# Attention, mixture of experts and feed-forward on one core: the first expert's first tile computed inside attention's last steps

## The chip, the cores and the metric

The kernel runs on one core of a Trainium2 chip. The metric is the device time of one execution in microseconds (us), the median of several runs. A core has five engines that run side by side, each through its own list of instructions in order: PE (TensorE, the matrix engine), DVE (VectorE), ACT (ScalarE), POOL (GpSimd) and SP (which here only issues transfers). They meet by semaphores. Transfers between the chip's memory and the core's on-chip memory go by 16 DMA engines.

## What is computed

The reference has three parts, one behind the other, cut here to what matters.

```python
# q, k, v: 4 batches, 8 heads, 576 positions, 64 wide
scores = scale * np.matmul(q, k.transpose(0, 1, 3, 2))
kth = np.partition(scores, -32, axis=-1)[..., -32:-31]
scores = np.where(scores >= kth, scores, -1e9)          # the 32 largest of each row
x = softmax(scores) @ v                                  # -> 2304 tokens x 512

do_compute = x @ w_skip > 0                              # the other tokens pass unchanged
e_idx = argmax(x @ w_gate); gate = its softmax           # one of 8 experts for each token
y = gate * (np.maximum(x @ w1[e], 0) @ w2[e])            # 512 -> 1024 -> 512
x[do_compute] += y

h = x @ w_in                                             # 512 -> 2048, weights in float64
out = (h / (1 + np.exp(-1.702 * h))) @ w_out             # 2048 -> 512
```

On the inputs of the reference the experts get 131, 62, 182, 117, 161, 178, 89 and 93 tokens.

## The kernel before

**Attention** is a software pipeline of 144 steps (`NTL`), nine to a pair of heads, sixteen pairs; a step works on one 128-row tile of scores, and its stages (scores, the top-32 threshold on VectorE, mask, transposes, the product with V, normalisation) run a few steps behind one another. The order of the instructions is the order in which the code of a step is written; nothing reorders them. Fourteen further steps (up to `NTL + AVL + 4`, `AVL` is 10) empty the pipeline. The gate of a batch (scores of the eight experts and of the skip weight, tile of 128 tokens by tile) is computed while the next batch is in work. The last batch has none behind it: `last_gate` computes its scores tile by tile in these last steps (transpose L547, copy L549, matmul L551, addition L553).

**Placing.** `rank` (L634, L636) counts on PE for each token how many tokens of its expert come before it. `place` (L642 on) turns that into a row and a column of a list, as one-hot rows `hr` and columns `hc`; `lists` (L703, first three batches, full lists) and `short_lists` (L716, last batch) multiply them on PE, so that each expert's list of token numbers comes out. `LST` collects the lists. For the last batch this is a serial chain between PE and VectorE, with the operations of `order` (the experts sorted by their number of rows, L787 to L812) woven between those of `place`, and nine matmuls on ones (`warm`, L259) on PE. When the first expert's list is there (L718, `IX0`), `first_rows` gathers its rows. Two tiles of 128 and 64 rows hold what an expert can have in the first five places (`BIGS`, "long", up to `NS` = 192 rows), one tile of 128 in the others.

**The flag.** `fine` (L927) is loaded by every engine from the on-chip memory: it is 1 if no expert has too many rows and no threshold was doubtful. Else an If (L1008) computes the lists exactly. Each engine waits behind the If until its branch is taken.

**Experts.** They run in the order of their places, `turns`, 0, 4, 1, 5, 2, 3, 6, 7, a long one and a short one by turns. Expert 0 is always in place 0 (its entry of `tie` is a large number). For an expert, `turn` (L1078) transposes the gathered rows; `layer1` (L1091) does 8 f x 4 fp32 matmuls, with ACT (L1092) and VectorE (L1094) splitting the hidden rows into a high and a low part; `split_w2` (L1136, L1137) splits the second weights likewise; `layer2` (L1109) does three fp32r matmuls for each f, or two where a tile has 64 rows (high and low part side by side); `scatter` writes rows back. Between the layers the next expert's rows are transposed, and the FFN's weights `w_in` are split in sixteen pieces (`split_f64`, L1033 to L1035 on VectorE): `take(e)` hands three pieces to a long expert's time, one to a short one's.

**The feed-forward part** (`L1264`, `L1279`) follows from about 619 us on.

Of the kernel before, what the change touches and what calls it, by code (L numbers as in the profile page):

```python
# [29 lines left out]
def body(ctx: ExitStack, tc: tile.TileContext, q, k, v, w_skip, w_gate, w1, w2, w_in, w_out, out):  # L30
# [82 lines left out]
    IXG = cst.tile([P, 2], I32, name="IXG")  # L113
    ZD = dram.tile([P, 8], F32, name="ZD")
# [6 lines left out]
    def first_rows(ready=False):  # L121
        w, src = (DM, X2D) if ready else (DM + 1, XD)
        if not ready:
            V.tensor_copy(IX0, IDX[:, :2])
            gate_places()
        fetch_rows(x0[0][:, :w], IX0[:, :1], src)
        fetch_rows(x0[1][: NS - P, :w], IX0[: NS - P, 1:], src)
# [4 lines left out]
    def first_gates():  # L132
        one = XD.rearrange("r (w o) -> (r w) o", o=1)
        fetch_rows(x0[0][:, DM:], IXG[:, :1], one)
        fetch_rows(x0[1][: NS - P, DM:], IXG[: NS - P, 1:], one)

    with ExitStack() as ph:
# [15 lines left out]
        IOF = X[:, 2 * P + LW + 8 : 2 * P + LW + 8 + 2 * E]  # L153
# [384 lines left out]
        def last_gate(r, u):  # L538
# [6 lines left out]
            zt, zg = SS[:, r * P : r * P + rows], SS[:rows, 1024 + 9 * r : 1033 + 9 * r]  # L545
# [52 lines left out]
        def gating_last(b):  # L598
# [24 lines left out]
            G.tensor_scalar(cb, wm, -float(NTT), float(E * NTT), op0=ALU.mult, op1=ALU.add)  # L623
# [15 lines left out]
        def place():  # L639
            b, cb = st.pop("fin")  # L640
            W = V if b == B - 1 else G
# [6 lines left out]
            W.tensor_tensor(acc, acc, MS[:, :5, :], op=ALU.mult)  # L648
# [6 lines left out]
            W.tensor_tensor(left, tk, pos, op=ALU.subtract)  # L655
            ad = gm.tile([P, 4, 5], F32, name="ad")
            W.tensor_scalar(ad[:, 0, :], pos, 1.0 / P, -0.498, op0=ALU.mult, op1=ALU.add)
            if W is V:
                yield
            W.tensor_scalar(ad[:, 0, :], ad[:, 0, :], 3.0 * 2.0 ** 22, 1.0, op0=ALU.add, op1=ALU.mult)  # L660
            if W is V:
                yield
            W.tensor_scalar(ad[:, 0, :], ad[:, 0, :], -3.0 * 2.0 ** 22, 1.0, op0=ALU.add, op1=ALU.mult)
            yield
            neg = gm.tile([P, 5], F32, name="neg")
            W.tensor_scalar(neg, ad[:, 0, :], -float(P), 0.0, op0=ALU.mult, op1=ALU.add)
            yield
            W.tensor_tensor(ad[:, 2, :], ad[:, 0, :], cb[:, :, 0], op=ALU.add)
            W.tensor_tensor(ad[:, 3, :], left, neg, op=ALU.subtract)
            W.tensor_tensor(ad[:, 1, :], neg, pos, op=ALU.add)  # L670
            if W is not V:
                yield
            hot = [gm.tile([P, P], F32R, name="hr", bufs=5) for t in range(5)]
            for t in range(3, 5):
                if W is V:
# [681 lines left out]
```

## Time and profile before

| | before |
|---|---|
| median of 3 runs | 1039.68 us (1033.44, 1039.68, 1041.09) |
| profiled execution, own time | 1033.63 us |
| its span in the trace | 1030.7 us |
| mean granted clock of PE | 0.988 |
| PE busy | 989.4 us (96%), 6499 matmuls |
| weight loads of PE | 842.9 us (82%) |
| DVE busy | 704.6 us (68%) |
| ACT busy | 593.1 us (58%) |
| POOL busy | 478.3 us (46%) |

A busy share is a mean over the stages, and the stages have different limits. A row of the timeline names start, length, engine, line, operation, the tile written and the tiles read, shapes and how many instructions it stands for; in brackets stands how long the engine idled before it and what ended that. [...] A plain fp32 matmul is two PE instructions in the trace, and an fp32r one is one. The execution's own time is 2.9 us longer than its span.

### The profile page before, as it was taken

Reading aid. Unit: us, or ns where it says so; the run is one execution under the profiler, and the core shown is the slowest. Engines: PE = TensorE matmul, PEld = TensorE weight load, DVE = VectorE, ACT = ScalarE, POOL = GpSimd, SP = SyncE. Lnnn points to the kernel's source line nnn. Section 1 sums busy time; section 2 is a strip of 40 time slices with the busy share of each in tenths; the row PEclk is TensorE's granted clock in tenths of the full one; section 3 lists DMA queues with packets and bytes.
Section 4 is the critical chain, followed back from the end, with each engine's and each line's share of the span. In section 5 each row is a group of like instructions: output and inputs, shape, how many; then the busy total and the mean of one; then the engine's idle time right before and its main releaser. Section 6 shows DMA issues by size and latency. Waiting matters only on the chain.

```text
span 1030.7 us, 20024 instructions
## 1 busy us (share of the span) xinstructions
PE 989.4 (96%) x6499; PEld 842.9 (82%) x6499; DVE 704.6 (68%) x3326; ACT 593.1 (58%) x1261; POOL 478.3 (46%) x598
## 2 busy tenths in 40 slices
PE   7999999999999999878999989999999999999998
PEld 4888888888888888757989877888888888888887
DVE  7999999999999999965898976653232323322222
ACT  6999999999999999823534533332222222222222
POOL 5788888978898879733765652220000000000000
PEclk9999999999999999998999999999999999999999
DMA  3121116161511151037889863312000200100000
GB/s 87 44 45 38 33 37 130 40 203 40 132 40 40 40 125 24 1 95 281 276 328 385 301 218 134 102 62 73 10 1 1 82 1 1 62 1 1 9 33 21
DMA packets 99010, 92.11 MB, mean 89 GB/s; under 512 B 71760, under 2 KB 71760, under 8 KB 98896
## 3 DMA queue, kind: packets, MB, share of 16 engines
q1 hardware_dynamic: 96704, 83.91, 26.8%
q0 software_dynamic: 1760, 5.25, 1.5%
q10 hardware_dynamic: 432, 1.57, 0.4%
q8 instruction: 53, 0.87, 0.4%
q14 instruction: 61, 0.50, 0.2%
HBM read 72.38 MB, written 17.32 MB: 87 GB/s over the span
## 4 chain that ended last, share of the span: by engine, by line
PE 71%; DVE 18%; DMA 4%; ACT 3%; issue 2%; POOL 1%; another core or an unknown queue 1%; SPq 0%; DVEq 0%; ACTq 0%; POOLq 0%
PE ph L1279 19%; PE py L1264 18%; PE Y L430 7%; DVE C L296 5%; PE SS L273 5%; PE pt L370 4%; DVE z L329 2%; DMA raw<-in_moe_w_in_dram 2%; PE ph L1091 2%; PE pt L371 2%; PE SS L275 2%; PE py L1109 2%; DVE w2l L1137 1%; PE Y L427 1%; PE SS L267 1%
## 5 line engine op out<-in xcount | busy, mean ns | idle before, releaser
L296 DVE MAX8 C<-s 128x8 f32<-128x72 f32 x1152 | 222.0, 220 | 2.2 <-ACT s L289 2.2
L324 POOL TENSOR_TENSOR z<-s,z 128x576 f32<-128x576 f32 x144 | 203.3, 1412 | 43.3 <-ACT z L319 41.1
L1267 DVE TENSOR_TENSOR g<-py,g 128x512 f32<-128x512 f32 (+1 forms) x80 | 51.1, 639 | 180.1 <-ACT g L1266 180.1
L1266 ACT ACTIVATE g<-py 128x512 f32<-128x512 f32 (+1 forms) x80 | 44.3, 554 | 166.9 <-PE py L1264 166.8
L430 PE MATMUL Y<-vn,AT 128*128 128x65 f32 x1024 | 121.3, 272 | 0.0
L430 PEld LDWEIGHTS Y<-vn,AT 128*128 128x128 f32 x1024 | 119.4, 192 | 0.0
L356 ACT ACTIVATE k<-s,th 128x576 bf16<-128x576 f32 x144 | 113.4, 788 | 5.6 <-DVE T L337 5.0
L1279 PE MATMUL ph<-woh,gh 128*128 128x512 f32 x288 | 112.6, 391 | 3.3 <-ACT gh L1269 3.3
L319 ACT ACTIVATE z<-s,T 128x576 f32<-128x576 f32 x144 | 113.0, 785 | 4.0 <-DVE T L312 1.8
L370 PE MATMUL pt<-ident,a 128*128 128x128 f32 x576 | 114.6, 279 | 0.8 <-issue 0.8
L1279 PE MATMUL ph<-woh,gl 128*128 128x512 f32 x288 | 112.5, 391 | 0.0
L1279 PE MATMUL ph<-wol,gh 128*128 128x512 f32 x288 | 112.5, 391 | 0.0
L351 POOL TENSOR_SCALAR a<-s,m 128x576 f32<-128x576 f32 x144 | 108.0, 750 | 1.5
L329 DVE MAX8 z<-z 128x8 f32<-128x576 f32 x144 | 107.0, 743 | 0.2 <-POOL z L324 0.2
L371 PE MATMUL pt<-far,k 128*128 128x128 bf16 x576 | 106.1, 220 | 0.6 <-ACT k L356 0.5
L359 ACT ACTIVATE AT<-pt 128x512 f32<-128x512 f32 x144 | 86.7, 602 | 8.5 <-PE Y L430 7.2
L370 PEld LDWEIGHTS pt<-ident,a 128*128 128x128 f32 x576 | 82.9, 144 | 6.3 <-issue 1.0
L1271 DVE TENSOR_TENSOR gl<-g,gh 128x512 fp32r<-128x512 f32 (+1 forms) x80 | 51.1, 639 | 52.4 <-ACT gh L1269 48.5
L1264 PE MATMUL py<-xh,wih 128*128 128x512 f32 (+1 forms) x320 | 81.1, 375 | 0.8 <-ACT xh L1298 0.8
L1091 PE MATMUL ph<-xgT,w1t 128*128 128x192 f32 (+1 forms) x512 | 75.8, 309 | 6.1 <-DVE hb L1094 5.4
L1091 PEld LDWEIGHTS ph<-xgT,w1t 128*128 128x128 f32 x512 | 74.1, 197 | 7.8 <-DVE hb L1094 6.5
L1269 ACT ACTIVATE gh<-g 128x512 fp32r<-128x512 f32 (+1 forms) x80 | 47.1, 589 | 56.6 <-DVE g L1267 56.6
(263 smaller groups left out, 2137.1 us busy)
## 6 DMA issues: line engine op xcount, KB each, us to landing
w1t<-in_moe_w_dram SPq DMA_DIRECT2D x8, 2048.0 KB
w<-in_moe_w_dram SPq DMA_DIRECT2D x64, 256.0 KB
raw<-in_moe_w_out_dram SPq DMA_DIRECT2D x16, 512.0 KB
raw<-in_moe_w_in_dram SPq DMA_DIRECT2D x13, 512.0 KB
out_dram<-ot SPq DMA_DIRECT2D x18, 256.0 KB
qn<-in_q_dram SPq DMA_DIRECT2D x32, 128.0 KB
kn<-in_k_dram SPq DMA_DIRECT2D x32, 128.0 KB
vn<-in_v_dram SPq DMA_DIRECT2D x32, 128.0 KB
```

The source lines that it names most:

```text
L296: V.max(C[:, g, :], s[:, g * SEG : (g + 1) * SEG])
L319: A.activation(z, d["s", c], AF.Sign, bias=T24[:, NTL + 6 - n : NTL + 7 - n], scale=-1.0 - 2.0 ** -20, accum_out=sg)
L324: G.tensor_tensor(z, d["s", c], z, op=ALU.mult)
L329: V.max(z8, d.pop(("z", c)))
L351: G.tensor_scalar(a[:, o : o + S], d.pop(("s", c)), -1.0, d.pop(("m1", c))[:, :1], op0=ALU.mult, op1=ALU.add)
L356: A.activation(d["k", r][:, o : o + S], d["s", c], AF.Relu, bias=d.pop(("th", c)), scale=-1.0)
L370: T.matmul(out, a, ident, is_transpose=True, start=True, stop=False)
L371: T.matmul(out, d["k", r][:, sl], far, start=False, stop=True)
L430: T.matmul(y[:, w * j : w * j + w], t[:, 4 * j + g, :], d["v"][:, g, j, :], start=False, stop=(j == 1 and g == 3))
L1091: T.matmul(ph_[:, :ns], w1t[:, c, f * P : (f + 1) * P], xgT[:, c, :ns], start=(c == 0), stop=(c == KC - 1))
L1264: T.matmul(phh[:, :n], lh[:, c, fs], rh[:, c, :n], start=(u == 0 and c == 0), stop=(u == 2 and c == KC - 1))
L1279: T.matmul(po[t], lh[:, ts_], rh[f], start=(f == 0 and u == 0), stop=(f == FC2 - 1 and u == 2))
```

## The change

1. Expert 0's first tile is filled from the first three batches alone: 105 rows of them; what the last batch adds to expert 0 goes to its second tile, since the count is raised to 128 (`early_rows`). Its rows are gathered while attention still runs, transposed in step `NTL + 4`, and taken through the first layer (L826) in the steps up to `NTL + 13` and through the second layer (L833) before and behind `rank`, all in plain fp32 with the weights as loaded. `early_out` adds the result; its rows are scattered at the start of the MoE. There expert 0 has only its tile of 64 rows left.
2. `place_last` replaces `place` for the last batch, with fewer operations; the list columns of all five tiles come from two instructions (128x80) instead of one for each. The third batch's lists (L703) are made some steps earlier.
3. `order` and the last check stand behind the index of the first rows instead of among the placing; the flag's load follows `order` and `early_out`.
4. The nine matmuls on ones around `rank` are gone.
5. Expert 1 always takes the last place (its `tie` is -1e6) and runs second; its first weights are loaded in step 90. The order of places is 0, 7, 1, 4, 2, 3, 5, 6.
6. The sixteen pieces of `w_in` are split 1, 2, 3, 2, 3, 3, 2, 0 over the experts, where it was 3, 1, 3, 1, 3, 3, 1, 1.

```diff
+        def place_last():
+            b, cb = st.pop("fin")
...
+            V.tensor_scalar(neg, pos, float(P), -float(P), op0=ALU.is_ge, op1=ALU.mult)
+            V.tensor_tensor(row, neg, pos, op=ALU.add)
...
+            V.tensor_tensor(hf, IOR[:, : 2 * E].unsqueeze(1).to_broadcast(every), col.unsqueeze(2).to_broadcast(every), op=ALU.is_equal)
+            V.tensor_tensor(hf, hf.bitcast(F32), val.unsqueeze(2).to_broadcast(every), op=ALU.mult)
+            for t in range(3):
+                V.tensor_scalar(hrs[t], IOR[:, :P], row[:, t : t + 1], None, op0=ALU.is_equal)
...
         V.memset(tie[:, :1], 1.0e6)
+        V.memset(tie[:, 1:2], -1.0e6)
...
+        def early_rows():
+            V.tensor_scalar(base[:, :1], base[:, :1], float(P), None, op0=ALU.max)
+            V.tensor_scalar(IXA, LST[:, :1], padf, None, op0=ALU.add)
+            V.tensor_scalar(IXB, LST[:, :1], padf, float((B - 1) * S - 1), op0=ALU.add, op1=ALU.min)
+            fetch_rows(x0[0], IXB, XD[: (B - 1) * S, :])
+            yield
+
+        EZ = SS[:, 1024:]
+
+        def early_turn():
+            for c in range(KC):
+                T.transpose(EZ[:, c * P : (c + 1) * P], x0[0][:, c * P : (c + 1) * P], ident)
...
+            for f in range(FC1):
+                z = EZ[:, f % 4 * P : (f % 4 + 1) * P]
+                for c in range(KC):
+                    T.matmul(z, w1t[:, c, f * P : (f + 1) * P], st["ex"][:, c * P : (c + 1) * P],
+                             start=(c == 0), stop=(c == KC - 1))
+                yield
+                if f % 4 == 3:
+                    A.activation(st["eh"][:, (f - 3) * P : (f + 1) * P], EZ, AF.Relu)
+                    yield
+            for f in range(FC1):
+                T.matmul(EZ, st["eh"][:, f * P : (f + 1) * P], raws[f], start=(f == 0), stop=(f == FC1 - 1))
+                yield
+
+        def early_out():
+            V.scalar_tensor_tensor(x0[0][:, :DM], EZ, x0[0][:, DM:], x0[0][:, :DM], op0=ALU.mult, op1=ALU.add)
...
+        EARLY = {4: 1, 5: 1, 6: 1, 7: 1, 8: 2, 9: 2, 10: 1, 11: 2, 12: 1, 13: 1}
...
+            if n == NTL * 5 // 8:
+                w1u = load_w1(1)
...
-        warm(2)
+        next(eg)
         rank()
-        warm(7)
-        pg, og = place(), order()
...
+        for _ in range(4):
+            next(eg)
+        place_last()
         short_lists(0)
+        for _ in eg:
+            pass
         short_lists(1)
         first_rows(True)
-        for _ in og:
+        check(2)
+        for _ in order():
             pass
         short_lists(2)
         st.pop("hot")
         sort_lists()
         gate_places()
+        early_out()
         fine = nc.values_load(flags[:, 1:2], min_val=0, max_val=1)
...
-        turns = [0, 4, 1, 5, 2, 3, 6, 7]
+        turns = [0, E - 1, 1, 4, 2, 3, 5, 6]
+        MORE = [1, 2, 3, 2, 3, 3, 2, 0]
...
-            gs = [todo.pop(0) for _ in range(3 if turns[e] < BIGS else 1)]
+            gs = [todo.pop(0) for _ in range(MORE[e])]
...
-            ns = NS if long else P
+            ns = NS if long else P if e else NS - P
```

On PE, the end of attention before: `xb` is the last batch's normalised rows, `W` the gate's weights, `ones` a tile of ones, `MS` the chosen experts; the rows run from the third batch's lists to the first of the nine matmuls on ones.

```order
L547 MATMUL SS<-ident,xb_155 128x128
L828 MATMUL SS<-ident,GOOD 1x128
L703 MATMUL Z<-hc,hr 128x144 x5
L551 MATMUL SS<-W_92,z 128x9
L433 MATMUL pt<-vn_182,AT 128x130 x4
L434 MATMUL pt<-vm_184,AT 128x130
L525 MATMUL Z<-W_92,xt 128x9 x2
L547 MATMUL SS<-ident,xb_155 128x128
L547 MATMUL SS<-ident,xb_155 128x64
L551 MATMUL SS<-W_92,z 128x9
L551 MATMUL SS<-W_92,z 64x9
```

The same place of the changed kernel: `s` is the transposed early tile and then its hidden rows, `w1t` expert 0's first weights, `w_0` and on its second ones.

```order
L546 MATMUL SS<-ident,xb_157 128x128
L881 MATMUL SS<-ident,GOOD 1x128
L826 MATMUL SS<-s,w1t 128x128 x8
L550 MATMUL SS<-W_92,z 128x9
L826 MATMUL SS<-s,w1t 128x128 x4
L431 MATMUL pt<-vn_184,AT 128x130 x4
L432 MATMUL pt<-vm_186,AT 128x130
L523 MATMUL Z<-W_92,xt 128x9 x2
L546 MATMUL SS<-ident,xb_157 128x128
L826 MATMUL SS<-s,w1t 128x128 x4
L546 MATMUL SS<-ident,xb_157 128x64
L550 MATMUL SS<-W_92,z 128x9
```

The list matmuls L703 have left this place, and matmuls of the early first layer stand between the gate's; eight more (f0 and f1) stand ahead of these rows, and eight (f6 and f7) behind them, ahead of the last gate matmul. Then, still on PE, comes what leads to the index and the flag, first of the changed kernel from its last count matmul of `rank` on:

```order
L635 MATMUL Z<-MS,ones 128x8
L833 MATMUL SS<-w_2_3998,s 128x512
L833 MATMUL SS<-w_3_4000,s 128x512
L833 MATMUL SS<-w_4_4002,s 128x512
L833 MATMUL SS<-w_5_4004,s 128x512
L729 MATMUL Z<-hc,hr 128x16 x5
L833 MATMUL SS<-w_6_4006,s 128x512
L833 MATMUL SS<-w_7_4008,s 128x512
L986 TENSOR_LOAD flags
L1067 COMPARE_AND_BRANCH
```

Before, seven matmuls on ones stood between `rank` and the list matmuls, and two ahead of `rank`, where the second layer's w_0 and w_1 are now. On DVE, what stands from the first expert's index (`IX`) to the branch of the If, before:

```order
L718 SCALAR_TENSOR_TENSOR IX_105<-Z,padf,LST 128x2
L805 CAST flags<-GOOD 1x1
L807 TENSOR_TENSOR flags<-over,base 1x8
L809 TENSOR_TENSOR kept<-at_place,expert_no 1x64
L812 TENSOR_REDUCE flags<-kept 1x8
L720 SCALAR_TENSOR_TENSOR IDX<-Z,padf,LST 128x8x2
L816 TENSOR_TENSOR least<-at_place,IDX 128x128
L819 TENSOR_REDUCE IXS<-least 128x16
L130 TENSOR_SCALAR IXG<-IX_105 128x2
L927 TENSOR_LOAD flags
L1008 COMPARE_AND_BRANCH
```

and in the changed kernel, from the same index to the row where the two orders meet again:

```order
L731 SCALAR_TENSOR_TENSOR IX_105<-Z,padf,LST 128x2
L883 TENSOR_REDUCE GOOD<-SS 1x1
L884 TENSOR_SCALAR GOOD<-GOOD 1x1
L840 TENSOR_TENSOR rnk<-base,tie 128x8
L842 TENSOR_TENSOR above<-rnk 128x64
L844 TENSOR_REDUCE rnk<-above 128x8
L846 TENSOR_TENSOR at_place<-rnk,place_no 128x64
L848 TENSOR_SCALAR over<-rnk 1x8
L850 SCALAR_TENSOR_TENSOR over<-over,base 1x8
L852 TENSOR_REDUCE most<-over 1x1
L854 TENSOR_SCALAR most<-most 1x1
L856 TENSOR_TENSOR flags<-most,GOOD 1x1
```

Eleven operations have moved behind the index; the eight of before (L805 to L130) follow them unchanged, then `early_out` (128x512) and the load of the flag.

## Rows read from the trace of the kernel before

**Rows 1.** Busy time by stretch; columns: stretch, length, engines (instructions), PE clock, DMA share, GB/s.
```profile
415.00:441.60 26.60, 21.29 (x190) 18.52 (x186) 25.23 (x151) 21.10 (x46) 20.98 (x28) 1.00 0.00 1
441.60:452.10 10.50, 10.44 (x92) 9.75 (x92) 5.54 (x23) 2.90 (x6) 1.69 (x5) 1.00 0.14 54
452.10:456.40 4.30, 2.11 (x13) 1.34 (x14) 3.15 (x18) 0.24 (x1) 0.00 (x0) 1.00 0.75 268
456.40:461.60 5.20, 4.55 (x18) 1.97 (x17) 4.35 (x31) 0.00 (x0) 1.90 (x4) 0.67 0.73 131
461.60:467.30 5.70, 0.00 (x1) 0.04 (x1) 1.56 (x9) 0.00 (x0) 2.03 (x2) 0.66 0.29 82
...
505.60:597.00 91.40, 88.46 (x517) 80.06 (x517) 82.37 (x137) 41.76 (x96) 55.49 (x44) 1.00 0.91 330
```

**Rows 2.** Timeline of PE in the last full stretch of attention.
```profile
442.90 1.90 PE L430 MATMUL Y<-vn,AT 128*128 128x65 f32 x16
444.63 0.28 PE L370 MATMUL X<-ident,a 128*128 128x128 f32 x1
...
449.65 0.76 PE L703 MATMUL Z<-hc,hr 128*128 128x144 f32 x5
450.28 0.39 PE L551 MATMUL SS<-W,z 128*128 128x9 f32 x2
```

**Rows 3.** Timeline of PE from the last gate matmul to the lists.
```profile
454.45 0.28 PE L551 MATMUL SS<-W,z 128*64 128x9 f32 x2 [0.39 <-DVE z L549]
...
456.39 0.18 PE L634 MATMUL Z<-MS,upper 128*128 128x48 bf16 x1 [1.11 <-DVE MS L617]
...
460.85 0.74 PE L716 MATMUL Z<-hc,hr 128*128 128x16 f32 x3 [0.18 <-DVE hc L683]
```

**Rows 4.** Timeline of PE's weight loads, a 512-column fp32 pair in attention.
```profile
419.91 0.19 PEld L267 LDWEIGHTS SS<-kT,qb 128*128 128x128 f32 x1 [0.24 <-issue]
420.34 0.19 PEld L267 LDWEIGHTS SS<-kT,qb 128*128 128x128 f32 x1 [0.24 <-issue]
```

**Rows 5.** Groups by line over the span: busy, mean ns, idle before.
```profile
L359 ACT ACTIVATE AT<-pt 128x512 f32<-128x512 f32 x144 | 86.7, 602 | 8.5 <-PE Y L430 7.2
```

**Rows 6.** Timeline of DVE: first of `order`, its flag, the first expert's index.
```profile
457.15 0.17 DVE L787 TENSOR_TENSOR rnk<-base,tie 128x8 f32<-128x8 f32 x1
...
458.92 0.15 DVE L803 TENSOR_TENSOR flags<-most,GOOD 1x1 int32<-1x1 f32 x1
...
461.63 0.22 DVE L718 SCALAR_TENSOR_TENSOR IX<-Z,padf,LST 128x2 int32<-128x2 f32 x1 [0.43 <-PE Z L716]
```

**Rows 7.** DVE's queue in lines 927 and 1008: ns min/median/max, first and last start.
```profile
L927 DVEq TENSOR_LOAD <-flags x1: 548/548/548, 462.9 to 462.9; - x1
...
L1008 DVEq EVENT_SEMAPHORE  x2: 21/21/21, 467.0 to 467.1; - x2
...
L1008 DVEq COMPARE_BRANCH x1: 72/72/72, 463.6 to 463.6; - x1
```

**Rows 8.** Timeline of PE in expert 0 and the second expert's first layer.
```profile
467.30 1.70 PE L1078 MATMUL pt<-ident,xg 128*128 128x128 f32 x8 [5.71 <-remote]
469.60 12.66 PE L1091 MATMUL ph<-xgT,w1t 128*128 128x192 f32 x64 [0.60 <-ACT xgT L1080]
...
477.71 4.55 PE L1091 MATMUL ph<-xgT,w1t 128*128 128x192 f32 x27
482.10 0.60 PE L1078 MATMUL pt<-ident,xg 128*128 128x128 f32 x4
482.45 0.48 PE L1109 MATMUL py<-w2h,hb 128*128 128x512 f32 x1
...
491.62 7.70 PE L1091 MATMUL ph<-xgT,w1t 128*128 128x128 f32 x64
499.16 0.99 PE L1078 MATMUL pt<-ident,xg 128*128 128x128 f32 x8
```

**Rows 9.** What PE waited for in the last expert: us, times, longest.
```profile
PE ph L1091 <- DVE hb L1094: 3.5, 1, 3.5
```

More of the change, by code (lines that the diff above doesn't have):

```diff
@@ L113, in body @@
     IXG = cst.tile([P, 2], I32, name="IXG")
+    IXA = cst.tile([P, 1], I32, name="IXA")
+    IXB = cst.tile([P, 1], I32, name="IXB")
     ZD = dram.tile([P, 8], F32, name="ZD")
@@ L544, in last_gate @@
             xt = st["lx"][:, r * P : r * P + rows]
[L545 removed]
+            z0 = r % 4 * P
+            zt, zg = SS[:, z0 : z0 + rows], SS[:rows, 512 + 9 * r : 521 + 9 * r]
             if u == 0:
@@ L689, in place @@
-            st["hot"] = hot
-            if W is V:
-                st["ad"] = ad
+            G.tensor_tensor(ad[:, 2, :], ad[:, 0, :], cb[:, :, 0], op=ALU.add)
+            G.tensor_tensor(ad[:, 3, :], left, neg, op=ALU.subtract)
+            G.tensor_tensor(ad[:, 1, :], neg, pos, op=ALU.add)
+            yield
+            hot = []
+            for t in range(5):
+                hr = gm.tile([P, P], F32R, name="hr", bufs=5)
+                V.tensor_scalar(hr, IOR[:, :P], ad[:, 1, t : t + 1], None, op0=ALU.is_equal)
+                yield
+                hot.append((hr, full(ad, t)))
+                yield
@@ L723, in full_lists @@
         def full_lists():
+            b, pos, cb = st["last"]
+            ad = gm.tile([P, 4, 5], F32, name="ad")
+            tile_of(V, ad[:, 0, :], pos)
+            V.scalar_tensor_tensor(ad[:, 1, :], ad[:, 0, :], -float(P), pos, op0=ALU.mult, op1=ALU.add)
+            V.scalar_tensor_tensor(ad[:, 2, :], cb[:, :, 0], 0.5 * NTT, ad[:, 0, :], op0=ALU.mult, op1=ALU.add)
+            V.tensor_tensor(ad[:, 3, :], tokf[:, b, :], ad[:, 1, :], op=ALU.subtract)
             hot = []
@@ L879, in body @@
                 fresh.append(todo[-1])
-            elif i == 0 and "hot" in st:
+            elif st.pop("listed", i == 0 and n < SOON and "hot" in st):
                 live.append(lists(1))
-            live += [some(g, 3 if g in fresh or n >= NTL else 1) for g in todo]
+                if n > SOON:
+                    live.append(early_rows())
+            live += [some(g, 3 if g in fresh or n >= NTL + 4 else 2 if n >= SOON else 1) for g in todo]
             fresh.clear()
@@ L897, in body @@
                 check(CHECKS.index(n))
+            for _ in range(EARLY.get(n - NTL, 0)):
+                next(eg, None)
             if i == 8 and "fin" in st:
                 rank()
-            elif i == 8 and "hot" in st:
+            elif "hot" in st and (i == 8 if n < SOON else i != 5 and "listed" not in st):
                 next(lists(0))
+                if n >= SOON:
+                    st["listed"] = True
         for g in todo:
@@ L1015, in body @@
                     again(bv)
+                V.tensor_copy(IXA, padf)
+                V.tensor_scalar(IDX, LST, padf, None, op0=ALU.add)
+                spill(0, 0)
             V.tensor_scalar(IDX, LST, padf, None, op0=ALU.add)
@@ L1025, in body @@
             first_rows()
-        st.pop("ad")
+        st.pop("last")
     def split_f64(pool, src, hi, lo, queue=SY):
@@ L1128, in scatter @@
             )
-        late = []
+        late = [(IXA, x0[0][:, :DM])]
         spare = []
```

111 lines of the change are left out of this document (53 added, 58 removed).

## The prediction

> **What bounds the kernel now.** I read the busy time of each engine by stretch first, because the shares of the whole span mix stages with different limits. The attention before 441.6 us is bound by VectorE: DVE is busy for 25.23 of 26.60 us in its last stretch, PE for only 21.29. From 441.6 to 452.1 PE is the bound, with 10.44 of 10.50 us. From 452.1 to 467.3 nothing is full: PE works 2.11 of 4.30 us, then 4.55 of 5.20, and then nothing for 5.70 us. Behind it the mixture of experts (MoE) is bound by PE again, 88.46 of 91.40 us; the DMA engines come close there with a share of 0.91 [rows 1].
>
> I then followed PE in order of time. In the PE-bound stretch a 128x65 fp32 matmul takes 0.108 us: sixteen of them lie between 442.90 and 444.63. The five list matmuls of the third batch (L703) hold PE for 0.63 us, from 449.65 to 450.28 [rows 2]. Between the stages a serial chain runs: last gate matmul 454.45, rank 456.39, while PE passes its time with matmuls on ones that only keep it awake [rows 3]. On VectorE the placing follows; the index list IX comes at 461.63, the load of the flag at 462.9 [rows 6, 7]. The branch of the If is issued at 463.6 and VectorE arrives behind it at 467.0 to 467.1; PE's first transpose of the MoE starts at 467.30 [rows 7, 8]. So the way out of attention is a chain: last gate, rank, lists, index, flag, branch. What comes earlier in it moves everything behind it one for one, since PE idles until 467.30.
>
> **The change part by part.** The sum is made against the profiled execution, span 1030.7 us and own time 1033.63. The median of the runs shown, 1039.68, is 6.05 us above that; I add the sum's difference to it. No input reaches the If's body (the count of rows stays below every limit), so that the altered exact path costs nothing on the way.
>
> (a) Early first layer. Expert 0's first tile needs 8 f of 4 fp32 matmuls; each counts as two PE instructions, 64 in all. A 128x128 one is shown in the MoE: 64 instructions from 491.62 to 499.16, or 0.118 us each [rows 8]. By the order, f0 to f4 stand ahead of the last V matmuls, in the stretch that PE fills: 5 x 8 x 0.118 = 4.7 us. The list matmuls L703 leave it for an earlier place where DVE is the bound, -0.63. Since there is no idle time to hide them [rows 1], I take +4.1. Bounds: 0 if they fill waits that the early insertion itself makes, 4.7 if L703's place is not free. The four transposes of the gathered rows and the copies on ACT stand earlier, under VectorE, at nothing (0.5 us without that cover).
>
> (b) Up to rank. f5 fits into the 2.19 us for which PE idles between 452.1 and 456.4 [rows 1]. f6 and f7 (16 x 0.118 = 1.9) stand ahead of the last gate matmul; it idled 0.39 before [rows 3] and about 0.15 is slack of f5, so the gate is 1.35 late. Then PE, in order, waits for a relu over 128x512 on ACT (0.60, the mean of L359's operations of that size [rows 5]) and does two second-layer matmuls of 128x512 in plain fp32. Their pace stands in attention: weight loads of such a pair are 0.43 apart, two to a matmul, 0.86 each [rows 4]. So gate to rank is 0.60 + 1.72 = 2.3 instead of 1.94 (454.45 to 456.39); the gating chain itself gets shorter, since the two operations on GOOD leave it, and hides under them. With 0.3 for two hand-overs: 1.35 + 0.4 + 0.3 = +2.0. Bounds 1.0 (f6 hidden too) and 3.5 (none hidden, relu late).
>
> (c) Rank to index. Before 456.39 to 461.63, 5.24 us [rows 3, 6]. After, rank (0.15), four second-layer matmuls 4 x 0.86 = 3.44, then five list matmuls (1.2, by 0.78 for the last three from 460.85 to 461.63 [rows 3, 6]): 4.8. VectorE's shorter chain (14 operations, most of them some 0.22 behind one another as between 457.15 and 458.92) is ready at about 3.4, so PE decides. -0.5, bounds -1.5 and +0.5.
>
> (d) The flag. Before, index to load takes 1.3 us (461.63 to 462.9). Eleven operations now stand between them that lay among the placing: nine of the order (457.15 to 458.92 and its last, 1.9) and two on GOOD (0.4). So 3.6, +2.3, and all of what stood behind the load moves: branch (0.7 after the load) and arrival (3.4 after the branch) [rows 6, 7]. The final multiplication over 128x512 is issued ahead of the load but need not end before it. I take +2.2. Bounds 1.0 (small operations overlap at half that pace) and 3.0 (the 128x512 one is waited for). The row of the branch shows 3.4 us between issue and arrival, and this I use. [...]
>
> (e) Expert 0 in the MoE. Before: 467.0 to 491.62, 24.6 us: transposes and copies to 469.60, 64 instructions of 192 columns to 482.10, the next expert's transposes, 40 of fp32r from 482.45 to 491.62 at 0.229 [rows 7, 8]. The first layer's later part runs at 4.39 / 27 = 0.163, so 10.4 at full pace; 2.1 of its 12.5 went to its start at the lower granted clock (0.66 in the stretch just ahead [rows 1]). After: arrival 0.26, one set of transposes and a copy 1.45, 64 of 64 columns at 0.108 = 6.9, the same 2.1 for the start, 0.35 transposes, 0.5 until the last hidden rows are split, 16 x 0.229 = 3.7: 15.2. -9.4, bounds -11 (clock cost halves with the shorter work) and -6 (weight splits of expert 0 on ACT and VectorE take their old time and PE waits).
>
> (f) The last expert. PE waits 3.5 us for hb there, behind the split of a piece of the FFN's weights on VectorE [rows 9]. The last take goes from one piece to none, so this goes; the pieces move to the second, fifth to seventh experts' time, where VectorE is close to full (82.37 of 91.40 [rows 1]); I leave 0.2 for a new stall. -3.3, bounds -3.5 and 0.
>
> (g) Under the DVE-bound part of attention come the third batch's list addition (0.3, by its matmuls' new place) and the index arithmetic of the early gather: +0.4, bounds 0 and 0.8. Loading the second expert's first weights in attention costs nothing there (DMA share 0.00 in its last stretch [rows 1]).
>
> Sum: 4.1 + 2.0 - 0.5 + 2.2 - 9.4 - 3.3 + 0.4 = **-4.5 us**. Span 1026.2, own time 1029.1; on the median 1035.2. The work done early comes back at nearly its price: 9.4 saved for some 7.8 paid in (a) to (d). What remains is mostly (f).
>
> **The rivals.**
> A. The clock. [...] If the idle spots before rank draw the lower level, six second-layer matmuls cost twice, 6 x 0.86 = +5.1; if the thinner start of expert 0 stays there too, 6.9 + 3.7 less the 2.1 counted, +8.5. The net is then +0.6 to +9.1: slower. It decides once more than 4.5 us of PE's path work are added by the lower level. Against it: the new matmuls are longer than the ones removed and close the idle time of 452.1 to 456.4.
> B. The last gap moves instead of going: VectorE is late with another hb. Net -4.5 + 3.2 = -1.3. For it speaks the share of VectorE; against it that this wait is the only large one of the last stretch.
> C. PE in (a) is not what the end waits for: the chain of softmax, V and gates has slack for it. Net -8.6. For it speaks that the gate chain behind is serial; against it 10.44 of 10.50.
> D. DMA. If the expert weights arrive no sooner, the 9.4 come back as waits: net up to +4.9. For it the share 0.91 at 330 GB/s; against it 2 MB less to load there, some 6 us at that rate.
>
> E. The flag is not what PE waits for: (d) falls away, net -6.7, because the gather of the rows or another engine's branch ends later than VectorE's. Against it: PE moved 0.2 to 0.3 us after VectorE's arrival [rows 7, 8].
>
> **How the numbers follow.** Chances: forecast 0.52, A 0.12, B 0.13, C 0.12, D 0.08, E 0.03. The forecast's own range by its terms is 1032 to 1038. The range of 1026 to 1041 takes in B with the upper bounds of (b) and (d), and below it C and the scatter of the runs shown (lowest 1033.44, 6 below the median); it leaves out the most of A and D. A measurement of this kernel tells about 1% (10 us) from no change. Faster by more needs C together with the good bound of (e), or a little of the forecast's tail: 0.11. Slower by more needs A in full, or D with bad bounds: 0.05. The same: 0.84.
>
> **What would show it.** (a) PE full between 441.6 and the last gate, that gate some 5 us later. (b), (c) the second-layer matmuls 0.86 apart, and rank to index near 4.8; 1.7 apart is rival A. (d) 3.6 from index to load, 4.1 from there to arrival, arrival near 475. (e) expert 0 ending 15 after it. (f) no wait of PE above 1 us in the last expert. The prediction is wrong if the early matmuls lengthen the path by under 2 or by over 6, or if (e) is worth less than 6.

## The result and the profile after

The changed kernel takes 1046.76 us, the median of 4 runs (1044.65 to 1050.19), against 1036.99 us for the kernel before beside it: ratio 1.0102, 95% interval 1.0055 to 1.0149. So it is slower by 1%, where 0.996 was forecast. Six more runs of the same kernel (`again`), beside the last experiments, gave 1048.27 and 1.0112 (1.0074 to 1.0149); 9 to 10 us above the kernel before were expected of them, and the medians are 11.7 apart. The three runs of before that the forecast started from had a median of 1039.68; in the sets of 23 and 31 runs below it lies between 1035.68 and 1037.39, so the forecast of 1035.2 stood some 3 us too high for a change of -4.5. The profiled execution took 1044.65 us, its span is 1042.9.

First part of the profile's page, of the changed kernel:

```profile
...
PE 996.3 (96%) x6546; PEld 847.4 (81%) x6546; DVE 703.2 (67%) x3313; ACT 593.5 (57%) x1263; POOL 477.4 (46%) x598
```

Nothing is to be seen in the shares. Three rows of PE split the span instead: the first transposes of the MoE, the start of the second expert's first layer, the start of the feed-forward part. The first two of before are in [rows 8], this is the third:

```profile
619.50 1.48 PE L1264 MATMUL py<-xh,wih 128*128 128x512 f32 x4 [0.81 <-ACT xh L1298]
```

The timeline of PE after, with the idle time ahead of a row and what ended it in brackets:

```profile
480.81 0.66 PE L1140 MATMUL pt<-ident,xg 64*128 64x64 f32 x4 [7.43 <-DVEq L1067]
482.14 13.91 PE L1155 MATMUL ph<-xgT,w1t 128*128 128x64 f32 x64 [0.67 <-DVE xgT L1144]
...
501.85 7.31 PE L1155 MATMUL ph<-xgT,w1t 128*128 128x128 f32 x64
510.23 0.63 PE L1140 MATMUL pt<-ident,xg 128*128 128x128 f32 x4 [1.07 <-DMA xg<-XD,IXS]
...
566.51 0.63 PE L1140 MATMUL pt<-ident,xg 128*128 128x128 f32 x4 [2.52 <-DMA xg<-XD,IXS]
...
633.59 1.48 PE L1330 MATMUL py<-xh,wih 128*128 128x512 f32 x4 [0.81 <-ACT xh L1364]
```

| stretch | before | after | difference | forecast |
|---|---|---|---|---|
| to PE's first transposes of the MoE | 467.30 | 480.81 | +13.5 | +8.2 |
| from there to the second expert's first layer | 24.3 | 21.0 | -3.3 | -9.4 |
| from there to the feed-forward part | 127.9 | 131.7 | +3.9 | -3.3 |
| sum | 619.50 | 633.59 | +14.1 | -4.5 |

The feed-forward part itself took 409.3 us instead of 411.2; in the profiled execution of before its last 100 us ran at a mean granted clock (a share of PE's full speed) of 0.98, where the change's ran at 1.00, so this is no gain of the change. All three stretches came out otherwise than forecast, each in its own way.

**Ahead of the MoE.** The timeline of PE, with the early first layer (L826) and second layer (L833) around the last gate's matmuls (L546, L550) and rank (L633):

```profile
453.31 0.31 PE L546 MATMUL SS<-ident,xb 128*128 128x128 f32 x1
453.45 0.27 PE L881 MATMUL SS<-ident,GOOD 128*1 128x128 f32 x1
453.56 1.95 PE L826 MATMUL SS<-s,w1t 128*128 128x128 f32 x16
...
456.97 1.16 PE L826 MATMUL SS<-s,w1t 128*128 128x128 f32 x8 [0.69 <-ACT s L830]
...
464.29 0.28 PE L550 MATMUL SS<-W,z 128*64 128x9 f32 x2 [0.39 <-DVE z L548]
465.45 1.98 PE L833 MATMUL SS<-w,s 128*128 128x512 f32 x4 [0.88 <-DVE g L552]
467.27 0.19 PE L633 MATMUL Z<-MS,upper 128*128 128x48 bf16 x1
...
467.43 3.68 PE L833 MATMUL SS<-w,s 128*128 128x512 f32 x8
470.54 1.02 PE L729 MATMUL Z<-hc,hr 128*128 128x16 f32 x5
```

and the timeline of DVE beside it:

```profile
455.55 0.29 DVE L548 COPY z<-SS 128x128 f32<-128x128 f32 x1 [2.41 <-PE SS L826]
...
458.22 0.17 DVE L552 TENSOR_TENSOR g<-g,SS 128x9 f32<-128x9 f32 x1 [2.29 <-PE SS L826]
...
471.60 0.22 DVE L731 SCALAR_TENSOR_TENSOR IX<-Z,padf,LST 128x2 int32<-128x2 f32 x1 [1.45 <-PE Z L729]
473.42 0.28 DVE L883 TENSOR_REDUCE GOOD<-SS 1x1 f32<-1x128 f32 x1 [1.60 <-PE SS L833]
```

The copy L548 reads what the transpose of 453.31 wrote, yet it starts only at 455.55, when the sixteen matmuls behind that transpose are done. They write other columns of the tile SS, from 1024 on (`EZ` in the change). The addition L552 waits likewise. GOOD's reduction (L883) reads what L881 had written at 453.45, and stands until 473.42, behind the last second-layer matmul. Each time a VectorE operation that is ready waits for PE work that has nothing to do with it.

**Expert 0.** Busy time by stretch: length, PE, PEld, DVE, ACT, POOL (instructions), granted clock, DMA share, GB/s, of the changed kernel:

```profile
...
485.00:500.00 15.00, 15.00 (x64) 14.29 (x64) 6.66 (x15) 5.22 (x15) 6.08 (x5) 0.50 0.63 195
500.00:510.00 10.00, 9.16 (x73) 8.61 (x71) 7.16 (x8) 7.56 (x18) 8.64 (x8) 1.00 1.01 358
```

PE has no gap from 482 to 500, and the granted clock stays at 0.50, the lower level in what follows, all that time: 13.91 us for 64 instructions, 0.217 each, twice the 0.108 of the forecast. Before, the same point of the kernel was back at 1.00 from 475 on, after PE's first transposes at 467.30:

```profile
470.00:475.00 5.00, 5.00 (x21) 5.00 (x21) 0.56 (x3) 1.35 (x4) 2.76 (x3) 0.63 0.81 270
475.00:480.00 5.00, 5.00 (x33) 5.00 (x32) 2.94 (x10) 3.20 (x9) 1.94 (x2) 1.00 1.01 384
```

**The other experts.** What PE waited for from 480 to 640, in us, times, longest, after:

```profile
PE pt L1140 <- DVEq L1067: 7.4, 1, 7.4
PE pt L1140 <- DMA xg<-XD,IXS: 5.1, 6, 2.5
PE ph L1155 <- DVE hb L1158: 1.8, 2, 1.2
...
```

The wait of 3.5 us for hb, the hidden rows [rows 9], is gone, and 5.1 us for gathered rows stand in its place, half of it at 566.51, followed by a clock of 0.81 from 565 to 570 and 0.84 from 570 to 575. From the fifth expert's first layer to the sixth's, where this falls, it is 25.75 us instead of 21.00: this one expert costs 4.75 us more, and the last one 1.6 less.

### The profile page after: what moved, and what is told of

Same layout as the page of the kernel before. It is cut to its first block, busy times and chain, and to the rows that moved or that the text cites. A ratio compares the mean times of both kernels' runs of the same rounds, so it can differ in the third digit from the quotient of the medians.

```text
span 1042.9 us, 20083 instructions
## 1 busy us (share of the span) xinstructions
PE 996.3 (96%) x6546; PEld 847.4 (81%) x6546; DVE 703.2 (67%) x3313; ACT 593.5 (57%) x1263; POOL 477.4 (46%) x598
## 5 line engine op out<-in xcount | busy, mean ns | idle before, releaser
L1155 PE MATMUL ph<-xgT,w1t 128*128 128x128 f32 (+2 forms) x512 | 76.2, 313 | 2.9 <-DVE hb L1158 1.8
L1330 PE MATMUL py<-xh,wil 128*128 128x512 f32 (+1 forms) x320 | 78.9, 368 | 0.0
```

Source lines behind the costliest of these rows:

```text
L1330: T.matmul(phh[:, :n], lh[:, c, fs], rh[:, c, :n], start=(u == 0 and c == 0), stop=(u == 2 and c == KC - 1))
```

## The experiments

Every ratio is against the kernel before, run on the same chip.

| run | what it is | median us (runs) | ratio | 95% interval |
|---|---|---|---|---|
| split | change, early accumulator in a tile of its own | 1044.14 (10) | 1.0061 | 1.0032 to 1.009 |
| wide128 | change, 128 columns in expert 0 | 1045.38 (10) | 1.0077 | 1.0045 to 1.0109 |
| eflag | change, flag early again | 1045.26 (10) | 1.0063 | 1.0033 to 1.0094 |
| pieces | change, pieces as before | 1046.45 (11) | 1.0061 | 1.0036 to 1.0085 |
| bflag | before, flag late | 1036.67 (10) | 1.0014 | 0.9985 to 1.0043 |
| nowarm | before, without the matmuls on ones | 1032.75 (10) | 0.9989 | 0.9964 to 1.0014 |
| sum1 | change with five repairs | 1034.07 (10) | 0.9976 | 0.9951 to 1.0 |
| sum2 | as sum1, two repairs otherwise | 1039.47 (10) | 1.0035 | 1.001 to 1.006 |
| again | the change once more | 1048.27 (6) | 1.0112 | 1.0074 to 1.0149 |
| sum3 | sum1, one piece to the feed-forward part | 1031.88 (12) | 0.9963 | 0.9941 to 0.9985 |
| bleft | before, one piece to the feed-forward part | 1029.01 (12) | 0.9931 | 0.9904 to 0.9958 |

The runs of one kernel scatter by 5 to 12 us, so the single repairs are read from stretches of the trace, and the times decide only for the sums.

### split: a tile of its own for the early layer

```diff
-        SS = pp.tile([P, 3 * 512], F32, name="SS")
+        pss = ExitStack()
+        SS = pss.enter_context(tc.tile_pool(name="psS", bufs=1, space=PSUM)).tile([P, 3 * 512], F32, name="SS")
...
-        EZ = SS[:, 1024:]
...
+            if n == NTL + 4:
+                pss.close()
+                psE = pss.enter_context(tc.tile_pool(name="psE", bufs=1, space=PSUM))
+                SS = psE.tile([P, 2 * 512], F32, name="SS2")
+                EZ = psE.tile([P, 512], F32, name="EZ")
```

> The changed kernel, but the early layer's accumulator is a PSUM tile of its own instead of the third bank of SS; instructions and their order stay. Theory: the copies (L548) and additions (L552) of the last gate, and GOOD's reduction (L883), wait for every matmul on SS that was issued ahead of them, the early ones included. Then the last gate matmul comes about 4 us earlier (near 460.3 instead of 464.29), GOOD's reduction follows the index at once (1.5 us earlier), and PE's first transposes of the MoE stand near 475.5 instead of 480.81: about -5 us of the time. Rival: PE is simply full with the early matmuls (0.118 us each): the last gate matmul stays at 464, and the time within 1 us of the changed kernel's.

The first transposes stand at 476.79 instead of 480.81, -4.0 where -5 was expected. Timeline of PE, split:

```profile
460.20 0.39 PE L551 MATMUL SS<-W,z 128*128 128x9 f32 x2
460.44 2.03 PE L825 MATMUL EZ<-s,w1t 128*128 128x128 f32 x16
462.40 0.28 PE L551 MATMUL SS<-W,z 128*64 128x9 f32 x2
463.16 1.98 PE L832 MATMUL EZ<-w,s 128*128 128x512 f32 x4 [0.47 <-ACT s L829]
464.98 0.19 PE L634 MATMUL Z<-MS,upper 128*128 128x48 bf16 x1
...
476.79 0.66 PE L1147 MATMUL pt<-ident,xg 64*128 64x64 f32 x4 [5.70 <-DVEq L1073]
```

In these rows no gate matmul waits for its copy (0.39 us ahead of the last one in the change), with the same instructions in the same order. So the waits came from the shared tile, which is the theory's part. The rival's part is that the last gate matmul is still 7.95 us later than before (462.40 against 454.45), because the early matmuls fill PE. GOOD's reduction follows the index at once: 469.45 behind 469.31.

### eflag and bflag: the flag's place, from both kernels

In eflag the operations of `order` are woven into `place_last` one by one, and the last check stands ahead of it:

```diff
-        def place_last():
+        def place_last(og):
...
+            next(og, None)
...
-        CHECKS = [NTL + AVL - 4, NTL + AVL - 2]
+        CHECKS = [NTL + AVL - 4, NTL + AVL - 2, NTL + AVL + 3]
...
-        place_last()
+        og = order()
+        place_last(og)
...
-        check(2)
-        for _ in order():
+        for _ in og:
```

> The changed kernel, but the order of the experts and the last check are woven into the placing again, as before the change, so that the flag is written behind the index. Theory: VectorE's load of the flag comes when the second layer's last matmul is done and early_out is issued, near 473.5 instead of 476.7; PE's first transposes 3.2 us earlier, time about -3. Rival: PE waits for something else at that place (its own branch, the gather): no change, or under 1 us.

Timeline of PE, eflag:

```profile
466.08 3.65 PE L842 MATMUL SS<-w,s 128*128 128x512 f32 x4 [1.63 <-ACT ex L609]
...
479.52 0.47 PE L1149 MATMUL pt<-ident,xg 64*128 64x64 f32 x4 [3.84 <-DVEq L1076]
480.66 13.92 PE L1164 MATMUL ph<-xgT,w1t 128*128 128x64 f32 x64 [0.67 <-DVE xgT L1153]
```

PE's idle time ahead of the first transposes falls from 7.43 to 3.84 us, but they come at 479.52, only 1.3 earlier where 3.2 were expected, and VectorE's load stands at 475.7 and not near 473.5. Rank comes 2.3 us later than in the change (469.57 against 467.27), for two reasons. The check now reads SS ahead of the second layer, which writes SS and starts after a wait of 1.63 us instead of 0.88; that this is the shared tile again is a reading of the order, since the profile names a row of ScalarE that the matmul does not read. And the first four instructions of the second layer take 3.65 us instead of 1.98: the granted clock is 0.51 from 466.08 to 469.57.

In bflag the kernel before gets the late order:

```diff
-        CHECKS = [NTL + AVL - 4, NTL + AVL - 2, NTL + AVL + 3]
+        CHECKS = [NTL + AVL - 4, NTL + AVL - 2]
...
-            if w < 6:
-                next(og, None)
-            if 1 < w < 5:
-                next(og, None)
...
         first_rows(True)
+        check(2)
         for _ in og:
```

> The kernel before, with one part of the change: the order of the experts and the last check stand behind the first expert's index. Theory: the load of the flag comes 3.6 us behind the index instead of 1.3, PE's first transposes 2.3 us later, all else moves along: time +2.3. The granted clock comes back about 5 us after PE resumes with 192 columns, as before. Rival: the longer idle time itself keeps the clock low for longer: first layer of expert 0 well above 12.7 us, time +4 or more.

Timeline of DVE and of PE, bflag, and DVE's load of the flag by its line:

```profile
469.68 0.22 DVE L718 SCALAR_TENSOR_TENSOR IX<-Z,padf,LST 128x2 int32<-128x2 f32 x1 [0.43 <-PE Z L716]
```
```profile
L924 DVEq TENSOR_LOAD <-flags x1: 543/543/543, 473.1 to 473.1; - x1
```
```profile
477.42 1.70 PE L1075 MATMUL pt<-ident,xg 128*128 128x128 f32 x8 [7.78 <-DVEq L1005]
479.72 13.58 PE L1088 MATMUL ph<-xgT,w1t 128*128 128x192 f32 x64 [0.60 <-ACT xgT L1077]
```

Index to load 3.4 us, index to first transposes 7.74 against 5.67: +2.1, the price that the prediction took. The first layer takes 13.58 instead of 12.66 after the longer idle time, so a little of the rival may hold (0.9 us). The time, +0.14% with an interval from -0.15 to +0.43%, can't tell +3 us from nothing.

### wide128: more columns in expert 0

```diff
+            while o < wide:
+                A.activation(xgT[:, :, o : o + rows], pt[:, :, :rows], AF.Copy)
+                o += rows
...
-                    T.matmul(ph_[:, :ns], w1t[:, c, f * P : (f + 1) * P], xgT[:, c, :ns], start=(c == 0), stop=(c == KC - 1))
+                    n1 = 128 if ns < P else ns
+                    T.matmul(ph_[:, :n1], w1t[:, c, f * P : (f + 1) * P], xgT[:, c, :n1], start=(c == 0), stop=(c == KC - 1))
```

> The changed kernel, but expert 0's first layer in the MoE multiplies 128 columns instead of 64 (the 64 rows twice). At full clock a 128-column matmul costs 0.118 us against 0.108, so +0.6 us of work. Theory: the granted clock stays at the lower level (0.50 from 480 to 500) because the matmuls are thin; with twice the columns it comes back after some 5 us, as before the change: first layer about 10 us instead of 13.9, second 3.7 instead of 5.5, time about -5. Rival: the clock stays low because PE idled 7.4 us ahead of it, whatever follows: first layer about 15 us, time +1.

Timeline of PE, wide128:

```profile
483.84 0.66 PE L1140 MATMUL pt<-ident,xg 64*128 64x64 f32 x4 [7.28 <-DVEq L1067]
485.58 9.55 PE L1159 MATMUL ph<-xgT,w1t 128*128 128x128 f32 x64 [1.08 <-ACT xgT L1147]
...
499.09 7.33 PE L1159 MATMUL ph<-xgT,w1t 128*128 128x128 f32 x64
510.47 1.71 PE L1140 MATMUL pt<-ident,xg 128*128 128x128 f32 x8 [4.05 <-DMA xg<-XD,IXS]
```

Busy time by stretch, columns as above, wide128:

```profile
484.00:490.00 6.00, 4.92 (x24) 4.73 (x24) 0.87 (x3) 1.72 (x5) 3.20 (x4) 0.50 0.41 134
490.00:499.00 9.00, 9.00 (x66) 8.37 (x65) 6.80 (x14) 4.61 (x13) 4.80 (x4) 0.99 0.71 236
```

Twice the work in columns takes 9.55 instead of 13.91 us, and the clock is back from 490 on, after the same idle time (7.28). Expert 0 lasts 15.25 us from the first transposes to the second expert (501.85 - 480.81 = 21.04 in the change). In eflag, with 64 columns after an idle time of only 3.84 us, the same 64 instructions took 13.92. There the clock stood at 1.00 from 470 to 479.5, right ahead of the MoE, and at 0.50 from 480 to 494.5. So in these runs the lower level goes with the 64 columns and not with the idle time ahead. Of the 5.8 us won here 1.9 are left when the third expert's first layer starts: PE waits 4.05 us at 510.47 (1.07 and 0.60 in the change), because the third expert's rows are not there. Their gather was issued at 501.49 and 502.77, while the DMA share is 0.97 and 1.03 from 500 to 511. At the feed-forward part 5.1 of the 5.8 are left, as the change loses more further on. The attention in this execution was 3 us longer at a lower clock (last section), which is why the first transposes stand at 483.84.

### pieces: the pieces of w_in as before

```diff
-        MORE = [1, 2, 3, 2, 3, 3, 2, 0]
+        MORE = [3, 1, 3, 1, 3, 3, 1, 1]
```

> The changed kernel, but the sixteen pieces of w_in are spread over the experts as before the change (3, 1, 3, 1, 3, 3, 1, 1). Theory: the 2.5 us for which PE waits in the fifth expert for the next rows' gather come from the second piece in the fourth expert's time, which GpSimd works on ahead of issuing the gather; wait and the lower clock behind it (0.81 and 0.84 from 565 to 575) go, about -4, and the last expert's wait for hb of 3.5 us is back, +2 to +3: time -1 to -2. Rival: the gather is late because the DMA engines are full (share above 1.0 there): the wait stays, the last expert's comes on top, +2 to +3.

What PE waited for from 480 to 632, pieces:

```profile
PE ph L1155 <- DVE hb L1158: 7.4, 3, 3.4
...
PE pt L1140 <- DMA xg<-XD,IXS: 0.7, 1, 0.7
```

The waits for rows go from 5.1 to 0.7 us, and the wait in the fifth expert with the lower clock behind it is gone, so the theory's half is right. The rival (a full DMA) falls, because the DMA share at this place is as high without the wait, 1.02, as it was with it in the change, 1.01 from 556 to 566.4. Busy time, columns as above, pieces:

```profile
555.00:564.40 9.40, 9.40 (x60) 9.40 (x59) 5.44 (x16) 5.94 (x14) 8.63 (x7) 1.00 1.02 384
```

GpSimd shows the mechanism; its timeline in the changed kernel, where PE waits until 566.51:

```profile
557.81 1.27 POOL L1101 TENSOR_TENSOR wil<-t,wih 128x512 fp32r<-128x512 f32 x1 [1.29 <-ACT wih L1100]
559.24 0.98 POOL L119 DMA_INDIRECT xg<-XD,IXS  x1 [0.15 <-issue]
560.52 0.92 POOL L119 DMA_INDIRECT xg<-XD,IXS  x1 [0.30 <-issue]
```

The gathers stand behind the second piece's last operation; in pieces, with one piece there, the first is issued at 556.51. What was not expected is the price on the other side: hb is waited for 7.4 us, 3.4 in the last expert as before, and another 3.35 in the second expert, where the three pieces taken in the shortened expert 0 now end up. The net, from the second expert to the feed-forward part, is 130.3 against 131.7 us.

### nowarm: the nine matmuls on ones

```diff
-        warm(2)
         rank()
-        warm(7)
```

> The kernel before without the nine matmuls on ones around rank, nothing else. Theory: they buy nothing that lasts, as the clock is at its lower level at 467 with them too: time within 1 us. Rival: they hold the clock up for the lists and for expert 0's start: without them the first layer of expert 0 stays at the lower level for longer, time +2 to +5.

The theory holds: 12.83 us for the first layer against 12.66, and the interval of the time takes in no change. The granted clock was 0.67 from 456.40 to 461.60 with the nine matmuls [rows 1] and 0.50 from 456.00 to 462.70 without them; through expert 0's first layer (467.30 to 482.10 and 468.70 to 484.00) it was 0.78 in both. Nothing shows a price for leaving them out.

### sum1, sum2 and sum3: the repairs together

sum1 is the change with split, eflag and wide128, the third expert's gather ahead of the loop (`nxt.append(gather(slots[2]))`), and `MORE = [2, 2, 3, 1, 3, 3, 2, 0]`. sum2 leaves the gather where it was and has `[1, 2, 3, 1, 3, 3, 3, 0]`. sum3 is sum1 with `[1, 2, 3, 1, 3, 3, 2, 0]`, fifteen pieces; the sixteenth is split in the feed-forward part:

```diff
+        wix = [fw.tile([P, DFF // 4], F32R, name=f"wix{i}") for i in range(2)]
+        over_piece = split_f64(wt, w_in[DM - P :, 3 * DFF // 4 :], wix[0], wix[1])
...
+                    own_ = c == KC - 1 and f >= 12
...
+                if b == 0 and f == 4:
+                    next(over_piece)
+                if b == 0 and f == 7:
+                    next(over_piece)
+                    next(over_piece)
```

> The changed kernel with five repairs: accumulator of the early layer in its own PSUM tile, order and check woven into the placing, 128 columns in expert 0's first layer, pieces 2, 2, 3, 1, 3, 3, 2, 0, and the third expert's rows gathered at the start. Theory: the single gains add, -4.0 (own tile), -3.3 (flag), -5 (columns), -4 (pieces), -1 (gather), so that the feed-forward part starts near 616 (619.5 before the change): time 2 to 4 us below the kernel before. Rival: the weights cannot come sooner; the gained time returns as waits for rows or weights in the second and third expert, feed-forward start at 620 or later, time at or above the kernel before.

> As sum1, but pieces 1, 2, 3, 1, 3, 3, 3, 0 and the third expert's rows gathered where the change does it. Theory: the third expert's gather lands late again behind the second expert's weights: PE waits some 4 us for it in the second expert, the rest as sum1, time 3 to 4 above sum1. Rival: the wait is hidden since PE has work until then: within 1 us of sum1.

> As sum1, but pieces 1, 2, 3, 1, 3, 3, 2, 0: the sixteenth piece of w_in goes to the feed-forward part, into two tiles of its own that only f 12 to 15 read. Theory: with one piece less in the experts' time the wait of 3.2 us for hb in the second expert goes and none takes its place, feed-forward start some 3 us earlier than in sum1 (616 where attention loses nothing to the clock), time 3 us below sum1, 4 to 6 below the kernel before. Rival: the wait in the second expert is for w2's splits, not for the piece: as sum1.

Timelines of PE around the second expert, sum1 and then sum3:

```profile
500.15 5.47 PE L1175 MATMUL ph<-xgT,w1t 128*128 128x128 f32 x32 [3.21 <-DVE hb L1178]
```
```profile
497.86 3.84 PE L1175 MATMUL ph<-xgT,w1t 128*128 128x128 f32 x32 [0.54 <-DVE hb L1178]
...
520.70 0.63 PE L1156 MATMUL pt<-ident,xg 128*128 128x128 f32 x4 [2.04 <-DMA xg<-XD,IXS]
```

sum1 is at the level of the kernel before or just below. Its feed-forward part starts at 622.72, about 619 without what attention lost to the clock in this execution (last section), where 616 was expected: two pieces in expert 0's time bring 3.2 us of waiting in the second expert. The rival was right that the gain comes back as a wait there, though it is a wait for hb and not for rows or weights. The early flag brought less too: VectorE's load now stands at 474.8 behind `early_out`, which needs the last second-layer matmul (474.73). In sum2 the third expert's rows are late by 2.3 and 0.7 us, and three pieces in the seventh expert make PE wait 3.9 us in the last one, which was not expected; sum2 is 5.4 us above sum1, for an expected 3 to 4. sum3 loses the wait of 3.2 us, as expected, but gets one of 2.04 for the fourth expert's rows (0.18 in sum1): from PE's first transposes to the feed-forward part it takes 142.3 us against 143.9 in sum1, 1.6 of the 3 us. It ends 4.7 us below the kernel before (medians 1031.88 and 1036.53), sum1 1.6 (1034.07 and 1035.68), but the intervals of the two overlap.

### bleft: the piece without the early tile

The same two tiles and the same split in the feed-forward part, in the kernel before, and no piece in the last expert:

```diff
-            gs = [todo.pop(0) for _ in range(3 if turns[e] < BIGS else 1)]
+            gs = [todo.pop(0) for _ in range(0 if e == E - 1 else 3 if turns[e] < BIGS else 1)]
```

> The kernel before with its sixteenth piece of w_in moved to the feed-forward part in the same way (3, 1, 3, 1, 3, 3, 1, 0), nothing else. Theory: the last expert's wait of 3.45 us and the lower clock behind it go without any early tile, time -3 to -4 against the kernel before. Rival: the next piece of work on VectorE there makes PE wait as long (in the changed kernel 1.24 and 0.70 us stay): -1 to -2.

Timeline of PE in the last expert and at the feed-forward part's start, bleft:

```profile
597.45 7.31 PE L1091 MATMUL ph<-xgT,w1t 128*128 128x128 f32 x64
...
615.49 1.47 PE L1269 MATMUL py<-xh,wih 128*128 128x512 f32 x4 [0.81 <-ACT xh L1303]
```

The 64 instructions run without a gap, the feed-forward part starts at 615.49 instead of 619.50, -4.0, of which 0.4 lie ahead of the MoE (first transposes at 466.88). The theory holds in the trace. The time, 0.9931 (0.9904 to 0.9958), is the best of all kernels, 2.9 us below sum3 in the medians. It is 7.5 us below the kernel before, with an interval from 4.4 to 10: more than the trace shows at this place, and where the rest comes from was not settled. So the one gain of the change that holds needs nothing of the early tile, and the early tile with every repair found here earns nothing beside it.

## Why the prediction was wrong

At the start of the feed-forward part the sum is off by 18.6 us (-4.5 forecast, +14.1 measured): 5.3 ahead of the MoE, 6.1 in expert 0, 7.2 behind it. The steps that failed are, by size, the 0.2 us left for a new stall in (f), the 2.1 us carried over for the start in (e), and in (a), (b) and (d) the waits: the prediction let an operation wait for what it reads and not for the whole tile.

The first stretch, term by term. The terms are differences between rows of before and after that answer to each other; "own tile" is split.

| term | forecast | change | own tile |
|---|---|---|---|
| start of the execution | 0 | +0.85 | +0.62 |
| (g) VectorE-bound end of attention | +0.4 | +1.27 | +1.30 |
| (a) 128x65 matmuls to the last V matmuls | +4.1 | +5.33 | +4.56 |
| (b) from there to rank | +2.0 | +3.43 | +2.11 |
| (c) rank to index | -0.5 | -0.91 | -0.91 |
| (d) index to first transposes | +2.2 | +3.54 | +1.81 |
| sum | +8.2 | +13.5 | +9.5 |

The start is a shift of all tiles from the fifth on that differs from execution to execution of every kernel (-0.3 to +2.4 us), and no part of the change.

(a) The price of the matmuls was right: L826 in attention costs 0.11 to 0.12 each, and PE had no room. Two things were missing. The half with f 4 to 7 writes where f 0 to 3 still stand, and waits for their relu (0.56 in split, 0.69 in the change); and the copies of the last gate wait for matmuls behind their transposes (0.8 us of the term). The prediction followed the order of the instructions and the durations, but took each operation to wait only for what it reads. What it waits for in this program is the last writer of the tile, as split shows.

(b) In split the term is 2.11 against 2.0: relu, two matmuls and the hand-overs were sized right. The change pays 1.3 more by the shared tile.

(c) The direction and the cause were right (PE decides); a second-layer matmul takes 0.78 instead of 0.86 us (4 in 3.11 us, 467.43 to 470.54).

(d) This is the term of which split and bflag show +1.8 and +2.1 for a forecast of +2.2. In the change, GOOD's reduction adds a wait of 1.60 that the prediction did not have. The arrival itself: branch issued at 477.4, arrival at 480.6, 3.2 us where [rows 7] have 3.4. The branch's own row on VectorE is 72 ns long, but PE waits for the arrival, and that came 2.9 to 3.5 us behind the branch in the kernels here. Between the two, from 477.4 to 480.6, the queues that the profile marks `instruction` moved five packets; what takes the 3.2 us was not shown.

(g) The term was mis-sized: 1.3 instead of 0.4. The list operations of the third batch now stand two to a step; that this is what stretches the VectorE-bound steps is a reading of the order, and no run tests it.

(e) The step of this term that failed is "the same 2.1 for the start". It carried over a cost in microseconds from matmuls of 192 columns to matmuls of 64. The other numbers of the term hold: with 128 columns expert 0 takes 15.25 us for a forecast of 15.2 less the arrival's 0.26. Rival A named the lower clock in this place and priced it, at twice the cost, at up to 8.5 us; it measured 5.8 (21.04 - 15.25), in expert 0 alone. The other half of rival A, the lower clock in the early second layer, did not come in the change: 0.78 us each, granted clock 1.00 from 452 to 470. In eflag it came, for the first two of the eight matmuls.

(f) Failed as rival B foresaw it, but by another way. The last wait was removed, and the pieces moved to other experts made new ones. The prediction looked for these on VectorE alone, and left 0.2 us for them. In the change the piece delays a gather, on GpSimd; in pieces, sum1 and sum2 it is hb, each time 2.5 to 3.9 us wherever the sixteenth piece stood. Term (f) left out that expert 0's own time shrinks (24.3 to 21.0 us, 15.25 with 128 columns) while its weights to split stay the same: the experts' time is shorter, and the sixteen pieces are not fewer.

Rival D may have a part: with wide128 the third expert's rows are late by 4.05 us at a DMA share of 0.97 to 1.03. That the share makes them late was not tested; with the gather issued at the start (sum1, sum3) PE does not wait for them. Rival C falls, PE was as full as the rows said. Rival E falls, PE moved right behind VectorE's arrival in each kernel (480.81 behind 480.6 to 480.7 in the change, 476.79 behind 476.6 to 476.7 in split).

What stays open: sum3 and bleft differ by 2.9 us in the medians, while their feed-forward parts start at nearly the same place once the shifts that the two executions had before the moved lists are taken off (620.53 less 3.8, 615.49 plus 0.4); how much of the 2.9 is the clock in attention, below, was not settled. The mean granted clock over the whole execution does not point that way: 0.983 to 0.995 in the runs of sum3, 0.981 to 0.991 in those of bleft, the faster of the two.

## What to carry to other kernels

Work that is put into the gaps of a serial chain must not share a tile with it: an operation of this program waits for the last writer of the tile, whatever part it reads (2.41 us ahead of the copy L548 in the change; with the early matmuls in a tile of their own the first transposes came 4.0 us earlier). A row whose bracket names a writer of another part of the tile, as SS L826 ahead of the copy L548, is the sign of it. Shortening a stage that hides other work (splits of weights, gathers, loads) moves that work, so price what the stage covered before counting what it loses. And before a large rearrangement, try the one wait it would remove by itself: here moving one piece to the feed-forward part gained 7.5 us in the medians, where 4.5 were forecast for the whole change.

## What the runs showed of the hardware

In the change a first layer of 64-column matmuls ran at a granted clock of 0.50 from its start to its end; PE was busy for all of the 15.00 us from 485 to 500, and the clock did not rise. In wide128 the same layer with 128 columns was at 0.50 until 490 and at 0.99 from there to 499.

Some executions lose 3 to 4 us to the lower clock inside attention, at a place where the kernel before runs at 1.00; sum1, with DVE idle beside it:

```profile
428.00:436.00 8.00, 8.00 (x45) 7.43 (x45) 4.81 (x34) 4.68 (x11) 2.45 (x3) 0.52 0.03 6
```

Three of the nine profiled executions with the moved lists have it there (0.53 from 428 to 436 in wide128, 0.52 in sum1, 0.50 in again), none of the four without them (one of those, bflag, has one at 444 to 460, 0.55 and then 0.50). Three more of the nine have a shorter one close by, at which the steps lose nothing that shows (0.57 from 419 to 423 in pieces, 0.66 from 423 to 428 in sum2 and sum3). With so few this shows no cause; it is a part of the scatter of the times.
